# A fused attention and feed-forward kernel: order of the first loads, TensorE turns of two tiles, four equal token blocks and a new written-out order of work

## The chip, the cores and the metric

One core of a Trainium2 chip runs the whole kernel. The time is the device time of one execution in microseconds (us), the median of several runs.

## The reference

One pre-norm layer on 2048 tokens of width 640, in bfloat16. `A` is a linear attention of 32 heads of 20 columns, whose features are softmaxes of a projection and of its negative; `B` is a feed-forward layer of width 1536 whose gate is a plain product.

```python
def _A_ref(x, wqkv, w_phi, wo):
    q, k, v = heads(x @ wqkv)
    pq = jnp.einsum("bhsd,hdf->bhsf", q, w_phi)
    pk = jnp.einsum("bhsd,hdf->bhsf", k, w_phi)
    phi_q = jnp.concatenate([_softmax(pq), _softmax(-pq)], axis=-1)
    phi_k = jnp.concatenate([_softmax(pk), _softmax(-pk)], axis=-1)
    kv = jnp.einsum("bhsf,bhsd->bhfd", phi_k, v)
    z  = jnp.einsum("bhsf->bhf", phi_k)
    num = jnp.einsum("bhqf,bhfd->bhqd", phi_q, kv)
    den = jnp.einsum("bhqf,bhf->bhq", phi_q, z)[..., None] + 1e-6
    return merge(num / den) @ wo
def _B_ref(x, w_gate, w_up, w_down):
    return ((x @ w_gate) * (x @ w_up)) @ w_down
h = x + _A_ref(_layernorm(x), A_wqkv, A_w_phi, A_wo)
h2 = h + _B_ref(_layernorm(h), B_w_gate, B_w_up, B_w_down)
```

## The kernel before

The 2048 tokens are 16 tiles of 128, and the width 640 is five blocks of 128. All weights and the residual stay on chip. The code builds a graph of about a thousand named steps; each step has an engine, buffers that it reads and writes, and one entry in a written-out table, `PLAN`.

**What sets the order.** An entry such as `WTe1:7.329:1` or `V2:20.248::2` holds a start key, the choice of engine (0 the first named for the step, 1 the other) and the buffer slots, PSUM banks for TensorE's outputs. `arrange` (line 700) sorts each engine's steps by the key, and `emit` (line 717) derives the semaphore waits from the buffers. An engine runs its steps strictly in that order, so a step that waits holds all that stand behind it on its engine. DMAs stand in the order of the engine that issues them, SyncE (SP) or ScalarE (ACT).

**The steps by name** (a number is the tile; the lines are those of the profile):

- `x`, `wk`, `wv`, `w5` and the like are loads (line 285). A block of `wk` or `wv` is 128 rows of the key or value weights, 160 KB; `x0` to `x3` are one tile each, later loads of `x` two tiles. `wqt` is a transposing load of the query weights (309). `wg`, `wu`, `wd` and `wo` are the later weights.
- `warm` (371): products of zeros on TensorE at the start.
- `WT` turns a block of the key weights on TensorE (392), `WTe` copies it out (251). `F1` multiplies it by the feature weights `Phi` (411), so that a projection and its feature product become one matrix; `Fe` copies it out. `F0` does this for the query weights later.
- `L1s`, `L1a`, `L1l`, `L1e`, `L1n`, `xn`: the first layer norm (428 to 453). `LNG` names the tiles that share one pair of Ln and Exp (436, 439). `xt` turns the normed tile: on TensorE for the tiles in `TPE` (462, copied out by `xte`), by a DMA transpose on SyncE for the others (471).
- `V`, `K`, `Q`: projections (482), ten products a tile; for the tiles in `TSPLIT` they are five pieces by block of the weights. `Kx`, `Ks`, `Kr`, `Ke`, `Kn` make the key features (494 to 518, `Kn` on GpSimd); `KV` adds a tile to the sums (526), `KVe` masks the sums. `Qx`, `Qs`, `Qr`, `Qb`, `Qe`, `Qn` make the query features (553 to 571), `qT` turns them by DMA (576).
- `N`: numerator and denominator (589). `dd`, `rd`, `o`: the division on VectorE (600 to 606). `oT`: turned by DMA (610). `O`: output projection (616). `h`, `L2s`, `L2a`, `L2v`, `L2r`, `hc`: residual and second layer norm (620 to 639). `hT`: turned by DMA (643).
- `U`: gate and up products of a token block, for each of 12 blocks of width 128 (658); `g` copies the gate (663), `u` multiplies (666). `D`: down projection of a tile (677); `y`: scale and residual (689); `w`: store (691).

`FB` lists the token blocks of the feed-forward part. A block's `U` products need the `hT` of all tiles in it. `LASTCUT` cuts the last tile's `D` into pieces of columns.

Of the kernel before, what the change touches and what calls it, by code (L numbers as in the profile page):

```python
# [8 lines left out]
ALU = mybir.AluOpType  # L9
AX = mybir.AxisListType  # L10

P = 128
# [26 lines left out]
FB = [(0, 256), (256, 512), (768, 512), (1280, 512), (1792, 256)]  # L39
LNG = [[0], [1], [2, 3], [4, 5, 6, 7], [8, 9, 10, 11], [12, 13, 14, 15]]  # L40
TPE = (0, 1, 2, 3)
TSPLIT = (0, 1)
NWARM = 10
LASTCUT = [(0, 320), (320, 512), (512, 640)]
# [4 lines left out]
x0:0.7:1 w5:1.18:1 wk0:1.18 wv0:4.06 wk1:2.14 wv1:2.62 wk2:1.66:1 wv2:3.58:1 wk3:2.62:1 wv3:4.06 wk4:3.1 wv4:4.54:1 x1:0.7 x2:2.14:1 x3:1.66 x4:3.58:1  # L49
x6:3.1 x8:5.02:1 x10:5.02 x12:4.54:1 x14:21.015 wqt0:13.874 wqt1:9.289 wqt2:26.055 wqt3:6.94 wqt4:19.655 wo0:27.415 wo2:34.715 wd0:35.195 wd1:47.175  # L50
wd2:49.392 wd3:37.595 wg0:32.875 wu0:5.5 wg1:37.115 wu1:6.46 wg2:40.335 wu2:25.575 wg3:36.635 wu3:5.98 wg4:35.675 wu4:36.155 id0:0.9 gl0:1.2 eps:0.7
id1:1.45 gla0:2.07 glb0:2.51 gla4:2.29 glb4:4.51 gla1:2.73 glb1:3.17 gla2:3.39 glb2:4.73 gla3:1.85 glb3:2.95 va1:6.664 phz:3.61 ekz:6.364 rqz:6.064
Sz:7.734 mk0:6.164 mk1:7.484 mk2:7.934 zero:0.7 warm0:1.08 warm1:1.51 warm2:1.94 warm3:2.37 warm4:2.8 warm5:3.23 warm6:3.66 warm7:4.09 warm8:4.52::0
warm9:4.74 Ph0:4.95 Ph1:5.609 Ph2:5.743:1 WT0:4.96::1 WTe0:5.509 WT1:6.769::5 WTe1:7.329:1 WT2:5.836::0 WTe2:6.386 WT3:7.725::2 WTe3:8.85 WT4:8.886::0
WTe4:9.922 F1_0:6.342::6 Fe1_0:8.676:1 F1_1:8.162::4 Fe1_1:9.299 F1_2:7.219::0 Fe1_2:8.052:1 F1_3:9.509::6 Fe1_3:10.766 F1_4:10.953::0 Fe1_4:11.538:1
L1s0:3.993 L1a0:5.633 L1s1:4.813 L1a1:6.1 L1s2:7.03 L1a2:9.686 L1s3:6.21 L1a3:10.215 L1s4:11.145 L1a4:12.785 L1s5:11.965 L1a5:13.005 L1s6:13.115
L1a6:14.353 L1s7:10.325 L1a7:12.895 L1s8:20.053 L1a8:21.803 L1s9:20.983 L1a9:23.833 L1s10:14.463 L1a10:20.873 L1s11:15.283 L1a11:19.443 L1s12:28.423
L1a12:34.233 L1s13:25.363 L1a13:30.243 L1s14:26.183 L1a14:34.123 L1s15:31.773 L1a15:34.013 L1l0:6.132 L1e0:7.229 L1l1:7.009 L1e1:7.952 L1l2:10.546
L1e2:11.389 L1n2:11.899 L1n3:11.699 L1l4:14.835 L1e4:15.678 L1n4:16.588 L1n5:16.188 L1n6:16.388 L1n7:15.988 L1l8:24.376 L1e8:24.806 L1n8:28.209
L1n9:28.409 L1n10:25.45 L1n11:25.65 L1l12:34.675 L1e12:35.518 L1n12:35.895 L1n13:36.095 L1n14:38.854 L1n15:36.295 xn0:7.85::0 xt0:8.53::3 xte0:9.268:1  # L60
xn1:8.35::1 xt1:9.165::1 xte1:9.796:1 xn2:12.875:1:3 xt2:17.252::7 xte2:17.978 xn3:12.161:1:2 xt3:13.17::0 xte3:13.935:1 xn4:19.553::2 xt4:21.495
xn5:17.025:1:0 xt5:18.295 xn6:18.943::1 xt6:22.855 xn7:23.333::3 xt7:24.215 xn8:29.243::1 xt8:30.155 xn9:29.743::3 xt9:31.515 xn10:26.408:1:0
xt10:27.895 xn11:27.745:1:2 xt11:33.355 xn12:36.631:1:0 xt12:45.815 xn13:36.758::1 xt13:38.075 xn14:39.692::2 xt14:47.712 xn15:38.118:1:3 xt15:40.815
V0_0:14.536::0 V0_1:14.807 V0_2:15.079 V0_3:15.351 V0_4:15.622 Ve0:20.238::2 K0_0:9.866::2 K0_1:10.138 K0_2:10.681 K0_3:12.083 K0_4:12.898
Kx0_0:13.588::0 Kx0_1:15.055 Ks0:16.103::0 Kr0:17.738 Ke0:18.601 Kn0:18.961 KV0:21.606::0,1 V1_0:12.355::6 V1_1:13.449 V1_2:13.721 V1_3:13.992
V1_4:14.264 Ve1:15.778::0 K1_0:10.41::4 K1_1:11.268 K1_2:11.54 K1_3:11.811 K1_4:12.626 Kx1_0:14.211::1 Kx1_1:16.401 Ks1:17.523::1 Kr1:19.998
Ke1:22.731 Kn1:23.091 KV1:26.01 V2:20.248::2 Ve2:22.108::3 K2:18.89::6 Kx2_0:21.485::3 Kx2_1:22.881 Ks2:23.943::3 Kr2:25.545 Ke2:28.458 Kn2:28.818
KV2:31.759 V3:15.894::2 Ve3:18.751::1 K3:17.531::4 Kx3_0:19.375::2 Kx3_1:20.861 Ks3:21.913::2 Kr3:23.513 Ke3:24.596 Kn3:25.85 KV3:33.747 V4:24.651::6
Ve4:27.121::5 K4:26.325::4 Kx4_0:28.608::0 Kx4_1:29.471 Ks4:30.353::1 Kr4:32.115 Ke4:32.978 Kn4:33.536 KV4:36.051 V5:21.935::4 Ve5:23.753::4
K5:23.293::2 Kx5_0:24.921::4 Kx5_1:25.785 Ks5:27.003::0 Kr5:29.231 Ke5:30.095 Kn5:31.177 KV5:36.367 V6:32.074::6 Ve6:33.811::7 K6:30.4::4  # L70
Kx6_0:32.355::3 Kx6_1:33.188 Ks6:34.343::3 Kr6:36.391 Ke6:37.968 Kn6:39.054 KV6:43.561 V7:29.042::6 Ve7:30.868::6 K7:27.684::2 Kx7_0:30.245::1
Kx7_1:31.491 Ks7:32.593::2 Kr7:34.435 Ke7:35.618 Kn7:36.495 KV7:43.876 V8:34.063::4 Ve8:35.768::2 K8:38.671::2 Kx8_0:40.299::0 Kx8_1:41.132
Ks8:41.966::1 Kr8:43.566 Ke8:44.634 Kn8:45.961 KV8:48.538 V9:44.463::4 Ve9:46.092::0 K9:36.997::6 Kx9_0:38.831::2 Kx9_1:39.665 Ks9:40.498::0
Kr9:42.379 Ke9:43.242 Kn9:43.602 KV9:51.842 V10:49.125::6 Ve10:51.708:1:3 K10:46.093::2 Kx10_0:48.562::3 Kx10_1:49.455 Ks10:50.288::3 Kr10:51.925
Ke10:52.788 Kn10:53.419 KV10:56.233 V11:54.874::2 Ve11:57.303:1:1 K11:40.029::4 Kx11_0:41.756::4 Kx11_1:42.619 Ks11:43.452::2 Kr11:45.647 Ke11:49.305
Kn11:50.82 KV11:59.265 V12:63.655::2 Ve12:65.321:1:4 K12:56.548::4 Kx12_0:58.176::0 Kx12_1:59.01 Ks12:59.843::1 Kr12:61.48 Ke12:62.583 Kn12:63.355
KV12:73.164 V13:60.939::4 Ve13:63.15:1:5 K13:50.484::2 Kx13_0:52.165::1 Kx13_1:52.998 Ks13:53.92::0 Kr13:56.436 Ke13:57.479 Kn13:57.839 KV13:73.479
V14:67.73::2 Ve14:69.782:1:7 K14:65.014::4 Kx14_0:66.642::3 Kx14_1:67.529 Ks14:68.362::3 Kr14:70.209 Ke14:70.659 Kn14:71.163 KV14:73.795 V15:70.447::6
Ve15:72.075:1:6 K15:59.58::2 Kx15_0:61.84::2 Kx15_1:62.733 Ks15:63.901::2 Kr15:65.742 Ke15:66.192 Kn15:67.259 KV15:74.11 KVe0:74.956 KVe1:74.696
F0_0:35.421::6 Fe0_0:36.006:1 F0_1:36.682::4 Fe0_1:37.345 F0_2:35.736::2 Fe0_2:37.258:1 F0_3:33.432::2 Fe0_3:34.895 F0_4:38.356::4 Fe0_4:38.941:1  # L80
Q0_0:41.387::6 Q0_1:41.659 Q0_2:41.931 Q0_3:44.192 Q0_4:45.822 Qx0_0:46.715::1 Qx0_1:47.758 Qs0:48.772 Qr0:50.882::1 Qb0:53.179 Qe0:53.622 Qn0:56.018
qT0:57.473::1 Q1_0:47.452::4 Q1_1:47.723 Q1_2:47.995 Q1_3:48.267 Q1_4:48.854 Qx1_0:50.078::2 Qx1_1:51.122 Qs1:52.46 Qr1:54.589::2 Qb1:55.778
Qe1:57.869 Qn1:60.438 qT1:61.893::2 Q2:53.516::6 Qx2_0:55.633::4 Qx2_1:56.676 Qs2:58.054 Qr2:60.436::0 Qb2:61.743 Qe2:62.463 Qn2:65.714 qT2:67.169::4
Q3:42.202::2 Qx3_0:43.831::0 Qx3_1:44.844 Qs3:45.857 Qr3:47.518::0 Qb3:48.32 Qe3:49.185 Qn3:49.515 qT3:50.97::0 Q4:62.297::6 Qx4_0:63.925::0
# [153 lines left out]
def build_graph():  # L238
# [679 lines left out]
```

## Time and profile before

| | |
|---|---|
| median of 3 runs | 274.34 us (274.33 to 274.36) |
| span of the profiled execution | 272.2 us; the page has no other time for it |
| TensorE busy | 266.0 us, 2103 products |
| VectorE busy | 171.0 us |
| ScalarE busy | 116.6 us |
| GpSimd busy | 73.9 us |
| read and written in HBM | 11.00 MB and 2.62 MB |
| granted TensorE clock | 1.000 |

The span runs from the first to the last instruction. A matmul's duration in the profile includes its way through the array, so durations of neighbours overlap; the distance between two starts, or a piece of the chain divided by its count, is what one product costs. DMA-issuing instructions do not count as busy, though they occupy their engine's queue.

### The profile page before, as it was taken

Reading aid. Unit: us, or ns where it says so; the run is one execution under the profiler, and the core shown is the slowest. Engines: PE = TensorE matmul, PEld = TensorE weight load, DVE = VectorE, ACT = ScalarE, POOL = GpSimd, SP = SyncE. Lnnn points to the kernel's source line nnn. Section 1 sums busy time; section 2 is a strip of 40 time slices with the busy share of each in tenths; the row PEclk is TensorE's granted clock in tenths of the full one; section 3 lists DMA queues with packets and bytes.
Section 4 is the critical chain, followed back from the end, with each engine's and each line's share of the span. In section 5 each row is a group of like instructions: output and inputs, shape, how many; then the busy total and the mean of one; then the engine's idle time right before and its main releaser. Section 6 shows DMA issues by size and latency. Waiting matters only on the chain.

```text
span 272.2 us, 5234 instructions
## 1 busy us (share of the span) xinstructions
PE 266.0 (98%) x2103; PEld 177.2 (65%) x2103; DVE 171.0 (63%) x315; ACT 116.6 (43%) x307; POOL 73.9 (27%) x107
## 2 busy tenths in 40 slices
PE   7899999999989999999999999999999999999996
PEld 2777787777776788775555877766444457544774
DVE  4999978788899999897186147843324022314423
ACT  2999998987766746012213332300332220023000
POOL 7227996899974133200000000000000000000000
DMA  7997999987548998964022001531100001100011
GB/s 201 375 265 162 176 264 313 234 157 108 107 78 160 147 185 110 165 130 98 0 48 48 2 1 43 100 95 43 31 0 2 0 0 51 48 0 0 26 48 55
DMA packets 66600, 27.76 MB, mean 102 GB/s; under 512 B 57744, under 2 KB 65296, under 8 KB 66576
## 3 DMA queue, kind: packets, MB, share of 16 engines
q1 hardware_dynamic: 64752, 25.30, 45.2%
q10 hardware_dynamic: 1824, 2.13, 2.3%
q8 instruction: 16, 0.26, 0.5%
q14 instruction: 8, 0.07, 0.1%
HBM read 11.00 MB, written 2.62 MB: 50 GB/s over the span
## 4 chain that ended last, share of the span: by engine, by line
PE 93%; ACT 3%; DMA 2%; ACTq 1%; issue 0%; DVE 0%; DVEq 0%
PE ps L658 38%; PE ps L482 23%; PE ps L677 19%; PE ps L616 8%; DMA ev<-in_A_wqkv_dram 2%; PE ps L526 2%; ACT ph L553 2%; PE ps L589 1%; PE ps L411 1%; ACTq L285 1%; PE ps L462 0%; ACT ph L554 0%; PE ps L392 0%; ACT L884 0%; DVE Wp L689 0%
## 5 line engine op out<-in xcount | busy, mean ns | idle before, releaser
L658 PE MATMUL ps<-xnT,Wgu 128*128 128x512 bf16 (+1 forms) x600 | 105.2, 336 | 0.0
L658 PEld LDWEIGHTS ps<-xnT,Wgu 128*128 128x128 bf16 x600 | 58.5, 98 | 44.2 <-DVE ev L666 0.4
L663 ACT ACTIVATE gt<-ps 128x512 bf16<-128x512 f32 (+1 forms) x60 | 30.5, 511 | 91.4 <-PE ps L658 74.0
L482 PE MATMUL ps<-Wp,xnT 128*128 128x320 bf16 (+1 forms) x480 | 68.6, 299 | 0.8 <-ACT ph L554 0.8
L666 DVE TENSOR_TENSOR ev<-ps,gt 128x512 bf16<-128x512 f32 (+1 forms) x60 | 32.8, 577 | 47.4 <-PE ps L658 34.0
L482 PEld LDWEIGHTS ps<-Wp,xnT 128*128 128x128 bf16 x480 | 45.6, 97 | 18.4 <-ACT ph L554 0.9
L677 PE MATMUL ps<-Wd,ev 128*128 128x320 bf16 (+2 forms) x396 | 53.7, 295 | 0.0
L677 PEld LDWEIGHTS ps<-Wd,ev 128*128 128x128 bf16 x396 | 38.0, 98 | 14.5
L518 POOL TENSOR_TENSOR ek<-ek,SR 128x1280 bf16<-128x1280 bf16 x16 | 37.6, 2357 | 6.7 <-ACT SR L503 6.6
L689 DVE SCALAR_TENSOR_TENSOR Wp<-ps,rs,x_all 128x640 bf16<-128x640 f32 (+3 forms) x18 | 14.5, 808 | 32.9 <-PE ps L677 32.7
L553 ACT ACTIVATE ph<-ps 128x300 bf16<-128x300 f32 x64 | 23.8, 442 | 7.9 <-PE ps L482 7.4
L630 POOL TENSOR_SCALAR ln<-mv 128x1 f32<-128x1 f32 x16 | 3.3, 210 | 84.6 <-DVE mv L629 73.4
L557 DVE TENSOR_REDUCE S<-ph 128x66 f32<-128x1320 bf16 x16 | 24.2, 1515 | 3.1 <-ACT ph L554 3.1
L498 DVE TENSOR_REDUCE SR<-ek 128x64 f32<-128x1280 bf16 x16 | 23.4, 1472 | 1.3 <-ACT ek L494 1.2
L616 PE MATMUL ps<-Wo,Wp 128*128 128x320 bf16 x160 | 23.9, 299 | 0.3 <-ACT RQ L567 0.3
L494 ACT ACTIVATE ek<-ps 128x640 bf16<-128x640 f32 x32 | 22.3, 714 | 2.7 <-PE ps L482 2.4
L571 POOL TENSOR_TENSOR ph<-ph,RQ 128x660 bf16<-128x660 bf16 x16 | 20.9, 1307 | 6.2 <-ACT RQ L567 6.2
L639 ACT ACTIVATE xn<-x_all,mv 128x640 bf16<-128x640 bf16 x13 | 10.7, 828 | 24.2 <-DVE mv L629 24.2
L616 PEld LDWEIGHTS ps<-Wo,Wp 128*128 128x128 bf16 x160 | 15.2, 98 | 6.6 <-issue 0.6
L620 DVE TENSOR_TENSOR x_all<-ps,x_all 128x640 bf16<-128x640 f32 x16 | 13.0, 813 | 4.5 <-PE ps L616 4.4
L606 DVE TENSOR_TENSOR o<-ps,sm 128x720 bf16<-128x720 f32 x16 | 14.2, 894 | 0.1
L428 DVE BATCH_NORM_STATS2 st<-x_all 128x6 f32<-128x320 bf16 x16 | 7.6, 472 | 3.3 <-DMA x_all<-in_A_x_dram 3.3
(63 smaller groups left out, 171.4 us busy)
## 6 DMA issues: line engine op xcount, KB each, us to landing
out_dram<-Wp SPq DMA_DIRECT2D x15, 160.0 KB, 1.8
Wgu<-in_B_w_up_dram SPq DMA_DIRECT2D x5, 384.0 KB, 9.7
Wgu<-in_B_w_gate_dram SPq DMA_DIRECT2D x5, 384.0 KB, 7.0
Wd<-in_B_w_down_dram SPq DMA_DIRECT2D x4, 480.0 KB, 6.3
x_all<-in_A_x_dram SPq DMA_DIRECT2D x3, 320.0 KB, 6.8
x_all<-in_A_x_dram ACTq DMA_DIRECT2D x3, 320.0 KB, 9.1
Wp<-in_A_wqkv_dram SPq DMA_DIRECT2D x4, 160.0 KB, 7.4
x_all<-in_A_x_dram ACTq DMA_DIRECT2D x3, 160.0 KB, 4.9
```

What stands on the lines that cost most here:

```text
L482: ins = e.matmul(pb(b, hb)[:, 0:n1 - n0], lhsT=T["xnT"][:, NC - 1 - c, P * t:P * (t + 1)], rhs=T["Wp"][:, POS[kind], c, n0:n1], start=(c = ...
L494: G.op("act", "%sx%d_%d" % (nm, t, s), lambda e, s=s, b=b, ek=ek: e.activation(out=T["ek"][:, ek.slots[0], 0:2 * D].rearrange("p (b h s f) ...
L498: G.op("dve", "%ss%d" % (nm, t), lambda e, ek=ek, sr=sr: e.tensor_reduce(out=T["SR"][:, sr.slots[0], 0, :], in_=T["ek"][:, ek.slots[0], 0: ...
L518: G.op("pool", "Kn%d" % t, lambda e, ek=ek, sr=sr: e.tensor_tensor(out=T["ek"][:, ek.slots[0], 0:2 * D].rearrange("p (h f) -> p h f", f=DH ...
L553: e.activation(out=o_, in_=i_.rearrange("p (g j f) -> p g j f", j=3, f=DH), func=AF.Exp, scale=1.0 - 2.0 * sg)
L557: G.op("dve", "Qs%d" % t, lambda e, t=t, ph=ph: e.tensor_reduce(out=T["S"][:, t, 0:66].rearrange("p (g k) -> p g k", k=6), in_=pv(ph).rear ...
L571: return e.tensor_tensor(out=v, in0=v, in1=T["RQ"][:, rq.slots[0], 1, 0:33].rearrange("p (g j) -> p g j", j=3).unsqueeze(3).to_broadcast([ ...
L616: ins = e.matmul(pb(b, hb)[:, 0:320], lhsT=T["oT"][:, oT.slots[0], c, :], rhs=T["Wo"][:, c, 320 * hb:320 * (hb + 1)], start=(c == 0), stop ...
L658: ins = e.matmul(pb(b)[:, 0:n], lhsT=T["Wgu"][:, gu, c, P * ft:P * (ft + 1)], rhs=T["xnT"][:, NC - 1 - c, o0:o0 + n], start=(c == 0), stop ...
L663: G.op("act", "g%d_%d" % (bi, ft), lambda e, pg=pg, gt=gt, n=n: e.activation(out=T["gt"][:, gt.slots[0], 0:n], in_=pb(pg)[:, 0:n], func=AF ...
L666: o_ = G.op("dve", "u%d_%d" % (bi, ft), lambda e, pu=pu, gt=gt, hh=hh, ft=ft, n=n: e.tensor_tensor(out=T["hh"][:, hh.slots[0], ft, 0:n], i ...
L677: ins = e.matmul(pb(b, hb)[:, 0:w], lhsT=T["hh"][:, hh.slots[0], ft, P * tt:P * (tt + 1)], rhs=T["Wd"][:, ft, c0 + w * hb:c0 + w * (hb + 1 ...
```

## The change

- The first loads get a new order: `x1`, `w5`, `x0`, `wk2`, `wk3`, `wk0`, `x2`, `wk4`, `wv0`, `wk1`, `wv1`, `x4`, `wv2`, `x3`, `wv3`, `wv4`, then `wqt1`, `x8`, `x6`. All but `x1` and `x0` are issued by SyncE; before, ten of the first twenty came from ScalarE. `wu0`, `wu3` and `wu1`, which stood among the first loads, come after 38 in the keys.
- `warm` becomes eight products of 512 columns and five of 256; four of the five stand before the first `WT`, the last between the first `WT` and `xt1`.
- `TPE` shrinks from four tiles to two: tiles 2 and 3 are turned by DMA.
- `FB` becomes four blocks of 512 tokens; before there were blocks of 256, 512, 512, 512 and 256.
- `LNG` has nine groups for six. `LASTCUT` cuts at 320 and 576, and the piece of 256 columns comes last.
- `L1n`, `Kn`, `Qb`, `Qn` and `L2v` may run on VectorE as well as GpSimd. `PLAN` moves to VectorE: `Kn12`, `Qn3`, `Qn9`, six `Qb`, five `L1n` and eight `L2v`. Some copies change between ScalarE and VectorE: four `xn` and three `hc` go to VectorE, four `Ve` and three `Fe0` to ScalarE.
- `PLAN` is written anew: keys, engines and slots of all steps. After the last `KV` (tile 15), TensorE's order is `Q7 N0 N1 Q13 N3 N2 N9 Q11 O0 O1 Q14 O3 O2 Q8 N5 Q15 O9 N4 Q12 N7`, then the first `U` of block 0 (tiles 0 to 3). SyncE's order there is `qT10 oT0 oT1 qT4 oT3 oT2 oT9 qT7 hT0 hT1 hT3 hT2`.

```diff
-FB = [(0, 256), (256, 512), (768, 512), (1280, 512), (1792, 256)]
-LNG = [[0], [1], [2, 3], [4, 5, 6, 7], [8, 9, 10, 11], [12, 13, 14, 15]]
-TPE = (0, 1, 2, 3)
+FB = [(0, 512), (512, 512), (1024, 512), (1536, 512)]
+LNG = [[0], [1], [2], [3], [4, 5], [6, 7], [8, 9], [10, 11], [12, 13, 14, 15]]
+TPE = (0, 1)
 TSPLIT = (0, 1)
-NWARM = 10
-LASTCUT = [(0, 320), (320, 512), (512, 640)]
+NWARM = 8
+NFILL = 5
+LASTCUT = [(0, 320), (320, 576), (576, 640)]
...
+    for k in range(NWARM):
+        G.op("pe", "warm%d" % k, lambda e, k=k: e.matmul(T["PS"][:, 512 * k:512 * (k + 1)], lhsT=T["zero"][:, 0:P],
+             rhs=T["zero"][:, :], start=True, stop=True), 0.43, LT, [z_b], [], -90,
+             before=[G.by["warm%d" % j] for j in range(k)])
     wm_b = Buf("pwarm", "psum")
...
+    for k in range(NWARM, NWARM + NFILL):
+        G.op("pe", "warm%d" % k, lambda e: e.matmul(pb(wm_b)[:, 0:256], lhsT=T["zero"][:, 0:P], rhs=T["zero"][:, 0:256],
+             start=True, stop=True), 0.22, LT, [z_b], [wm_b], -89, before=[G.by["warm%d" % j] for j in range(k)])
+    wall = [G.by["warm%d" % k] for k in range(NWARM)]
...
-                    op1=ALU.mult), 0.2, LP, [rs_b[t], mv_b[t]], [nb_b[t]], 10 * t - 25)
+                    op1=ALU.mult), 0.2, LP, [rs_b[t], mv_b[t]], [nb_b[t]], 10 * t - 25, alts=[("dve", 0.07, LD)])
...
-            pool_c(1280), LP, [ek, sr], [ek], kk)
+            pool_c(1280), LP, [ek, sr], [ek], kk, alts=[("dve", dve_c(1280), LD)])
...
-        G.op("pool", "Qn%d" % t, qn, pool_c(660), LP, [ph, rq], [ph], kk)
+        G.op("pool", "Qn%d" % t, qn, pool_c(660), LP, [ph, rq], [ph], kk, alts=[("dve", dve_c(660), LD)])
```

## The prediction

> **What bounds the kernel now.** I read the page's busy times first, then TensorE's products by shape, TensorE's waits, the chain in order of time, and the timeline of the first 18 us and of 74 to 96 us.
>
> The page's first part, and two rows of the groups by shape (busy us, mean ns of one, idle before):
>
> ```profile
> PE 266.0 (98%) x2103; PEld 177.2 (65%) x2103; DVE 171.0 (63%) x315; ACT 116.6 (43%) x307; POOL 73.9 (27%) x107
> ```
>
> ```profile
> L658 PE MATMUL ps<-xnT,Wgu 128*128 128x512 bf16 x360 | 79.0, 379 | 0.0
> L658 PE MATMUL ps<-xnT,Wgu 128*128 128x256 bf16 x240 | 26.5, 273 | 0.0
> ```
>
> TensorE is the bound. Its means are latencies that overlap, so prices come from the chain in order of time (start, us, what, count), where back-to-back products show their pitch:
>
> ```profile
> 14.25 0.28 PE ps L462 x5
> ...
> 95.83 13.18 PE ps L658 x120
> ...
> 121.30 2.16 PE ps L658 x10
> ...
> 164.03 0.68 PE ps L677 x12
> ...
> 222.06 13.04 PE ps L677 x96
> ```
>
> A 256-token product costs 13.18/120 = 109.8 ns, a 512-token one 216 ns, a turned tile 0.28 us, a 640-wide down projection 3.26 us, a Q, K, V or O projection 1.36 us, an N or KV step 0.33 us, a fold 0.32 us. All real work, at these prices, is 259.7 us. The last product ends at 269.7, so TensorE loses 10 us, in two places.
>
> The head, from the timeline; the third column of a wait is what ended it:
>
> ```profile
> 8.66 0.28 PEld L392 LDWEIGHTS ps<-ident,ev 128*128 128x128 bf16 x5 [0.36 <-DMA ev<-in_A_wqkv_dram]
> ...
> 9.89 0.28 PEld L392 LDWEIGHTS ps<-ident,ev 128*128 128x128 bf16 x5 [0.34 <-DMA ev<-in_A_wqkv_dram]
> ...
> 10.78 1.25 PE L482 MATMUL ps<-Wp,xnT 128*128 128x320 bf16 x8
> ```
>
> The key weights' blocks arrive one by one, the last at 9.85 (the trace's landing events). When projections begin at 10.78, 5 weight turns, 4 folds and 2 token tiles are done: 1.40 + 1.28 + 0.56 = 3.24. **Head loss: 10.78 - 3.24 = 7.54 us.**
>
> The stage between the last KV step and the first feed-forward product:
>
> ```profile
> 77.38 1.18 PE L589 MATMUL ps<-KVm,scratch 128*128 128x63 bf16 x33
> 79.35 2.91 PE L482 MATMUL ps<-Wp,xnT 128*128 128x300 bf16 x20 [0.80 <-ACT ph L554]
> ...
> 84.31 1.52 PE L616 MATMUL ps<-Wo,Wp 128*128 128x320 bf16 x10
> 86.13 1.52 PE L616 MATMUL ps<-Wo,Wp 128*128 128x320 bf16 x10 [0.29 <-ACT RQ L567]
> ```
>
> Three N steps from 77.38 need 1.00, the next projection starts at 79.35: 0.97 lost. O from 84.31 needs 1.36, the next starts at 86.13: 0.46 lost. With smaller gaps at 82.6 (0.16), 92.4 (0.13), 92.9 (0.20) and 95.7 (0.07): **2.0 us**. At 35.24 another 0.17 goes, and nothing after 95.74. From there the time is the sum of products.
>
> **The sum.** The profiled span is 272.2 and the runs' median 274.34: 2.1 us lie around the span. I add differences of the span to the median.
>
> *Feed-forward blocks.* 240 products of 256 tokens (26.35 us) become 120 of 512 (25.92): **-0.43**, certain, since TensorE never waits there. Copies and multiplies of 512 columns (597 and 683 ns) fit under the 2.16 us of their two products.
>
> *Two tiles leave TensorE.* Two of 0.28: **-0.56**. Their two copies (0.40 us pitch on VectorE, 0.58 on ScalarE) go too. In their place SyncE turns tiles 2 and 3; a row of 2.7 us from issue to landing shows that price when nothing is queued. Whether V2 waits for tile 2 belongs to the head.
>
> *First loads in use order.* Loads land about in issue order: the seventh block of 160 KB at 7.76, the eighteenth at 12.72, or 0.45 us each. The last turned key block (wk4) was twelfth and becomes seventh, so it lands near 7.8 instead of 9.85; the last one now is wk1, ninth, near 8.7. Then two folds that stand ahead of V1: 8.7 + 0.28 + 0.64, so projections begin near 9.7, when 5 turns, 2 tiles and 3 folds (2.92) are done. Loss 6.8 instead of 7.5: -0.75. Against it: x1 landed at 3.57 and still cannot come sooner; tile 2's turn stands on SyncE behind the first transposing load of the query weights and x8 and x6, and V2 wants it near 9.7 + 6.1 = 15.8. By 0.45 us a block, the sixteenth lands at 11.8, that transposing load and four more blocks at about 14.3, tile 2 some 1 us later: a wait of 0 to 0.5. I take **-0.5** for the head, bounds -0.9 and +0.5.
>
> Nearly all loads now go through SyncE's queue instead of half through ScalarE's. Fourteen issues at 0.47 us end at 7.4, and blocks drain at 0.45, so issue is never far behind. The Trainium skill ("DMA: Bandwidth & Descriptors", "Issuing engines are not separate DMA queues") says that issuing from several engines saves only the issuing time, since all run on the same 16 engines; the trace's interleaved landings agree, and by the rule the term stands.
>
> *Zero products.* Eight of 512 and four of 256 columns at half rate (427 and 213 ns) last as long as the ten before (4.27 us); the fifth small one costs 0.11 between turns, while TensorE waits for loads anyway. The head's gaps of 0.57 and 0.69 us left the pitch at 56 ns, so keeping TensorE busy buys nothing either: **0**. Without the cover: +0.11.
>
> *New order, 76 to 96 us.* The first feed-forward block now needs tiles 0 to 3, not 0 and 1. TensorE's work between the last KV step and that block: 7 Q (9.52), 5 O (6.80), 8 N (2.67) = 19.0 us. SyncE must issue eleven transposes for it (oT of five tiles, two qT, hT of four), at pitches of 1.33 (oT and hT) and 1.6 (qT) in these rows: ten ahead of the last take 13.8. The first oT can go 3.4 us after the last KV step (0.84 for the two masks, 0.33 for N, 2.2 for the division on VectorE), and the last hT lands 2.65 after issue: 3.4 + 13.8 + 2.65 = 19.9. So at least 0.9 us must be lost; I take 1.5 against 2.0: **-0.5**, bounds -1.5 and +2. VectorE matters here: it is busy 19.8 of 20 us in 80 to 100, and gets a copy (0.46) and three or four small operations (0.1 each) from ScalarE and GpSimd.
>
> *Small operations moved off GpSimd* (one Kn, two Qn, six Qb, thirteen of one column), and three more Ln/Exp pairs (0.28 each on ScalarE): no row shows Kn on VectorE. Its bounds are the 1.4 us that the `o` multiply's pitch (0.81 for 720 columns) gives and GpSimd's own 2.31; I take 2. All lies beside TensorE's projections with slots ahead: 0; if the cover is gone, one Kn holds VectorE for 2 us, and the next key step with it.
>
> *Query weights.* F0 follows V8 at about 31.4 now, not 34.4, and needs all five transposed loads. The last is issued after nine turns (1.3 each) and five loads (0.55 each) from 11.6, at 26.1, and landed 3.65 to 5.8 later in rows of its kind: 29.8 to 31.9. **+0.2**, bounds -0.2 and +0.5.
>
> *The end.* The last piece grows from 192 to 256 columns, the early one shrinks from 128 to 64. Twelve of 64 cost 0.36 (a 63-column product: 30 ns) to 0.68, of 256 1.32, of 192 about 0.99, of 128 0.68: equal sums. The last addition grows by about 0.07 and its store by 0.05: **+0.1**.
>
> Sum: -0.43 - 0.56 - 0.5 - 0.5 + 0.2 + 0.1 = -1.7: span 270.5, **time 272.6**.
>
> **Rivals.**
> A. *Early transposes stall SyncE* (slower). The timeline shows two transposing loads holding SyncE for 6.94 us in all (2.62 and 4.27, by the trace), with loads queued ahead:
>
> ```profile
> 8.09 6.94 SPq L309 DMA_TRANSPOSE scratch<-in_A_wqkv_dram  x2
> ```
>
> Now one such load and then tiles 2, 4 and 5 meet queued loads. If the first holds 2.6 and the second 4.3, tile 2's issue ends at 15.8 and lands at 17.2, V2 waits 1.4; tile 4, held 3.25, lands near 21 and V4 waits 1.1 more. That takes the head's term from -0.5 to +2.2: 275.3. It decides as soon as tile 2 lands after V2's turn at 15.8. Against it: then three up-projection blocks of 384 KB stood ahead, now four blocks of 160. Chance 0.10. The Trainium skill ("VectorE: DVE Perf Modes", "Rules for kernel authors") prefers TensorE for a 128x128 transpose into PSUM, at 390 ns there against 1309 by DMA; by those figures ten squares would be worth 3.9 us on TensorE, while the trace's two tiles cost 0.56.
> B. *Four tiles before the first block* (about the same). If SyncE's qT pitches are the longest of that stage (1.7 and more) or VectorE delays a division, 1.9 us more is lost there: 274.4, within 0.2% of before. Speaking for it: VectorE at 99%. Against: more Q work covers it. Chance 0.12.
> C. *The head is no shorter*: reordered loads land in the same crowd, gain 0; the rest stands: 273.1. Chance 0.18.
> Forecast itself: 0.60.
>
> **Range and chances.** 0.2% is 0.55 us, about what a measurement of this kernel can tell from no change. Forecast and C are faster by more: 0.78; B within: 0.12; A slower: 0.10. The bounds of head and stage together reach from 271.2 upwards; B's 274.4 is taken in, A left out: 271.2 to 274.5.
>
> **What would show it.** Right: first projection at 9.5 to 10; no waits of L482 on tile 2; the chain with 512-token products alone; TensorE's losses at 76 to 96 near 1.5; the last product near 268. Wrong: a wait of L482 on xnT's DMA at 15 to 20, of L411 on the query weights at 31, of L658 on xnT at its first product, or gaps of several tenths that recur through 20 to 73 us, where the old order lost only 0.17 and all engines are busy.

## The result and the profile after

**280.97 us** (median of 4 runs, 280.23 to 281.95) against 274.33 before on the same chip: the ratio is 1.0251, with a 95% interval of 1.0227 to 1.0275. The forecast was 272.6. The profiled execution took 281.95, the longest of the four, with a span of 280.2; I compare it with before's 272.2 and keep in mind that about 1 us of its 8.0 is this execution's own.

What the forecast called certain is there. The first part of the page after:

```profile
PE 267.9 (96%) x1976; PEld 165.3 (59%) x1976; DVE 182.7 (65%) x324; ACT 114.8 (41%) x300; POOL 67.9 (24%) x85
```

TensorE's products by shape, and a piece of its chain in order of time (start, us, what, count):

```profile
L651 PE MATMUL ps<-xnT,Wgu 128*128 128x512 bf16 x480 | 107.2, 379 | 1.1 <-DMA xnT<-xn 0.6 <-DVE sm L592 0.5
```

```profile
174.68 14.03 PE ps L651 x65
```

All gate and up products have 512 columns and cost 14.03/65 = 215.8 ns. But VectorE's busy time grew by 11.7 us, while the operations moved to it from GpSimd are some 6 us long when they run alone (the lengths are measured below); in this execution their rows add up to 14.1 us. This is the first thing to notice on the page. The second is where TensorE waits. Its waits (waited for: us, times, longest):

```profile
PE ps L474 <- ACT ek L486: 2.6, 1, 2.6
PE ps L474 <- DMA xnT<-xn: 2.5, 3, 1.0
...
PE ps L474 <- DVE ev L242: 0.8, 1, 0.8
PE ps L651 <- DMA xnT<-xn: 0.6, 1, 0.6
```

L474 is the projection (482 before), L242 a copy out of PSUM (251), L486 the exponential `Kx` (494): the last two hold a bank that the next projection needs. Before, projections lost 0.17 us between 20 and 73 us. TensorE's timeline shows the places; the bracket is the idle time ahead of a piece and what ended it:

```profile
9.20 1.25 PE L474 MATMUL ps<-Wp,xnT 128*128 128x320 bf16 x8
...
17.05 3.16 PE L474 MATMUL ps<-Wp,xnT 128*128 128x320 bf16 x22 [0.98 <-DMA xnT<-xn]
...
29.26 2.89 PE L474 MATMUL ps<-Wp,xnT 128*128 128x320 bf16 x20 [0.49 <-DMA xnT<-xn]
33.16 1.53 PE L474 MATMUL ps<-Wp,xnT 128*128 128x320 bf16 x10 [1.01 <-DMA xnT<-xn]
...
58.65 1.52 PE L474 MATMUL ps<-Wp,xnT 128*128 128x320 bf16 x10 [0.84 <-DVE ev L242]
...
73.33 7.29 PE L474 MATMUL ps<-Wp,xnT 128*128 128x300 bf16 x40 [2.61 <-ACT ek L486]
...
86.66 0.49 PE L581 MATMUL ps<-KVm,scratch 128*128 128x63 bf16 x11 [0.38 <-DVE sm L592]
...
90.48 1.52 PE L608 MATMUL ps<-Wo,Wp 128*128 128x320 bf16 x10 [0.38 <-ACT RQ L552]
```

Measured from start to start, as in the prediction: V1's pieces lose 0.61 us at 11 to 12.4 (they wait for the value weights), V2 1.15, V7 0.65, V8 1.18, K13 1.01 and Q6 2.77; the stage from 82 to 103 us loses 2.15 (2.0 before), and the second token block 0.78 at 137.6. After Q6's wait the products of 300 columns run at half rate for some 3 us, which costs 1.5 more. Projections begin at 9.20 with 2.92 us of work done, a head loss of 6.28 where it was 7.54.

**Balance.** Less work -1.0, head -1.26, waits behind the head +8.4 (10.5 now, 2.1 before), half rate +1.5: +7.6. The last product starts at 277.25 for 269.41, +7.84.

The same execution shows a cause for K13 and Q6. VectorE at 54 and 74 us, each time with GpSimd at the same time behind it:

```profile
54.45 0.60 DVE L445 TENSOR_SCALAR xn<-x_all,mv,rs 128x640 bf16<-128x640 bf16 x1
54.97 2.80 DVE L563 TENSOR_TENSOR ph<-ph,RQ 128x660 bf16<-128x660 bf16 x1
```

```profile
54.71 2.36 POOL L510 TENSOR_TENSOR ek<-ek,SR 128x1280 bf16<-128x1280 bf16 x1
57.02 1.91 POOL L563 TENSOR_TENSOR ph<-ph,RQ 128x660 bf16<-128x660 bf16 x1
```

```profile
73.58 1.47 DVE L490 TENSOR_REDUCE SR<-ek 128x64 f32<-128x1280 bf16 x1
74.97 3.42 DVE L510 TENSOR_TENSOR ek<-ek,SR 128x1280 bf16<-128x1280 bf16 x1
```

```profile
74.69 5.92 POOL L510 TENSOR_TENSOR ek<-ek,SR 128x1280 bf16<-128x1280 bf16 x2
```

Qn3 (54.97) and Kn12 (74.97) are two of the moved operations. Both begin beside a scaling on GpSimd, which ends at 57.07 (54.71 + 2.36) and 77.0; both end 0.7 and 1.4 us behind that, at 57.77 and 78.39. And GpSimd's next one, begun when the first ended, is longer by as much: Qn2 1.91 for its usual 1.31, and Kn15, the second of the last pair, about 3.6 (5.92 for the two) for 2.36. It looks as if the two engines exclude each other in operations with two inputs from SBUF, while a sum or a norm (one input) runs freely.

From there Q6's wait can be followed back. VectorE, then ScalarE:

```profile
66.46 2.47 DVE L563 TENSOR_TENSOR ph<-ph,RQ 128x660 bf16<-128x660 bf16 x1
68.85 1.29 DVE L556 TENSOR_TENSOR RQ<-RQ 128x32 f32<-128x32 f32 x1
```

```profile
70.17 0.23 ACT L559 ACTIVATE RQ<-RQ 128x32 f32<-128x32 f32 x1 [2.01 <-DVE RQ L556]
71.57 0.26 ACT L493 ACTIVATE SR<-SR 128x64 f32<-128x64 f32 x1 [1.17 <-DVE SR L490]
...
71.99 1.27 ACT L486 ACTIVATE ek<-ps 128x640 bf16<-128x640 f32 x2
```

Qn9 and Qb1, moved operations both, end late on VectorE; ScalarE has idled 2.01 us for Qb1's result, and behind that step stand Kr14 and, last, the exponentials of K15, which end at 73.27 and free the bank for Q6 at 73.33. K13's bank was freed by Ve10, which stood behind Qn3.

### The profile page after: what moved, and what is told of

It is laid out like the page before. It is cut to its first block, busy times and chain, and to the rows that moved or that the text cites. A ratio compares the mean times of both kernels' runs of the same rounds, so it can differ in the third digit from the quotient of the medians.

```text
span 280.2 us, 4952 instructions
## 1 busy us (share of the span) xinstructions
PE 267.9 (96%) x1976; PEld 165.3 (59%) x1976; DVE 182.7 (65%) x324; ACT 114.8 (41%) x300; POOL 67.9 (24%) x85
## 4 chain that ended last, share of the span: by engine, by line
PE 70%; DVE 14%; DMA 7%; ACT 6%; SPq 1%; issue 1%; DVEq 0%; ACTq 0%
PE ps L651 35%; PE ps L670 19%; PE ps L474 8%; DMA xnT<-xn 6%; PE ps L608 6%; DVE S L549 3%; ACT ph L545 3%; DVE SR L490 2%; DVE ph L563 2%; DMA ev<-in_A_wqkv_dram 1%; SPq L276 1%; ACT ek L486 1%; PE ps L581 1%; DVE x_all L612 1%; PE ps L518 1%
## 5 line engine op out<-in xcount | busy, mean ns | idle before, releaser
L651 PE MATMUL ps<-xnT,Wgu 128*128 128x512 bf16 x480 | 107.2, 379 | 1.1 <-DMA xnT<-xn 0.6
L651 PEld LDWEIGHTS ps<-xnT,Wgu 128*128 128x128 bf16 x480 | 46.4, 98 | 54.0 <-issue 1.5
L474 PE MATMUL ps<-Wp,xnT 128*128 128x320 bf16 (+1 forms) x480 | 71.2, 303 | 6.1 <-ACT ek L486 2.6
L656 ACT ACTIVATE gt<-ps 128x512 bf16<-128x512 f32 x48 | 28.0, 596 | 91.4 <-PE ps L651 66.2
L474 PEld LDWEIGHTS ps<-Wp,xnT 128*128 128x128 bf16 x480 | 45.8, 99 | 26.5 <-DMA xnT<-xn 4.4
L659 DVE TENSOR_TENSOR ev<-ps,gt 128x512 bf16<-128x512 f32 x48 | 31.9, 682 | 38.0 <-PE ps L651 23.1
L486 ACT ACTIVATE ek<-ps 128x640 bf16<-128x640 f32 x32 | 20.6, 699 | 1.4 <-PE ps L474 1.4
L563 POOL TENSOR_TENSOR ph<-ph,RQ 128x660 bf16<-128x660 bf16 x14 | 19.3, 1390 | 7.2 <-ACT RQ L559 7.2
L632 ACT ACTIVATE xn<-x_all,mv 128x640 bf16<-128x640 bf16 x11 | 9.1, 826 | 18.0 <-DVE mv L621 9.5
L556 POOL TENSOR_TENSOR RQ<-RQ 128x32 f32<-128x32 f32 x10 | 2.3, 238 | 38.1 <-ACT RQ L552 38.1
L622 POOL TENSOR_SCALAR ln<-mv 128x1 f32<-128x1 f32 x8 | 1.5, 211 | 40.6 <-DVE ln L622 26.3
```

The source lines that it names most:

```text
L474: ins = e.matmul(pb(b, hb)[:, 0:n1 - n0], lhsT=T["xnT"][:, NC - 1 - c, P * t:P * (t + 1)], rhs=T["Wp"][:, POS[kind], c, n0:n1], start=(c = ...
L486: G.op("act", "%sx%d_%d" % (nm, t, s), lambda e, s=s, b=b, ek=ek: e.activation(out=T["ek"][:, ek.slots[0], 0:2 * D].rearrange("p (b h s f) ...
L563: return e.tensor_tensor(out=v, in0=v, in1=T["RQ"][:, rq.slots[0], 1, 0:33].rearrange("p (g j) -> p g j", j=3).unsqueeze(3).to_broadcast([ ...
L651: ins = e.matmul(pb(b)[:, 0:n], lhsT=T["Wgu"][:, gu, c, P * ft:P * (ft + 1)], rhs=T["xnT"][:, NC - 1 - c, o0:o0 + n], start=(c == 0), stop ...
L656: G.op("act", "g%d_%d" % (bi, ft), lambda e, pg=pg, gt=gt, n=n: e.activation(out=T["gt"][:, gt.slots[0], 0:n], in_=pb(pg)[:, 0:n], func=AF ...
L659: o_ = G.op("dve", "u%d_%d" % (bi, ft), lambda e, pu=pu, gt=gt, hh=hh, ft=ft, n=n: e.tensor_tensor(out=T["hh"][:, hh.slots[0], ft, 0:n], i ...
```

## Experiments

There are three theories: **P**, the exclusion; **D**, transposes that land late behind loads; **R**, the new order leaves GpSimd's chain (16 `Kn` of 2.31 us, with `Qn` and `Qb` between) no slack, so that whatever delays it delays the last `KV`. A ratio is to the kernel before in the same job, in brackets its 95% interval. The start of KVe0, the mask on the finished key-value sums, serves as a mark of GpSimd's chain: 76.45 before, 82.04 after. GpSimd's idle time from the start of its first `Kn` to the end of its last is a second mark: 6.1 us before, 13.1 after. The rows of `Kn`, before and after, show how much GpSimd idles right ahead of a `Kn`, the first one included (last figure):

```profile
L518 POOL TENSOR_TENSOR ek<-ek,SR 128x1280 bf16<-128x1280 bf16 x16 | 37.6, 2357 | 6.7 <-ACT SR L503 6.6
```

```profile
L510 POOL TENSOR_TENSOR ek<-ek,SR 128x1280 bf16<-128x1280 bf16 x15 | 36.4, 2439 | 9.8 <-ACT SR L495 9.8
```

The runs were made on several chips; on these the kernel before took 274.09 to 274.75. The diffs below show only the entries and lines that matter. Places in time come from one profiled execution of each kernel.

### Undoing parts of the change

**e1.** The nine operations back on GpSimd.

```diff
-Kn12:67.028:1 Qn3:51.438:1 Qn9:60.309:1 Qb0:57.282:1
+Kn12:67.028 Qn3:51.438 Qn9:60.309 Qb0:57.282
```

(and Qb1, Qb8, Qb9, Qb13, Qb15 likewise)

> The changed kernel with nine two-input operations (Kn12, Qn3, Qn9, six Qb) back on GpSimd; all else, keys and slots too, as changed. Theory P: these operations on VectorE wait for whatever two-input operation GpSimd is in, so VectorE runs late from 55 us on; TensorE's waits of 1.0 us at 58.7 and 2.8 us at 73.3, and the half-rate products behind the second (1.7 us), come from that. P expects 275.5 to 277.5, no TensorE gap over 1 us between 50 and 80, and a granted clock of 1.00 at 70 to 80. Theory D: late DMA turns at 17, 29 and 33 us (3.0 us together) push everything behind; D expects that the time stays within 1 us of 281, since those waits stay. Theory R, the new order is too tight for GpSimd as well as for VectorE: the waits at 55 to 80 move to other steps and less than 2 us is gained.

Measured 282.26, 1.0284 [1.0239, 1.0329]: no gain, rather a loss. Q6 waits 1.20 for 2.77 and its products run at full clock, but K12, KV12 and KV15 now wait 0.79, 1.10 and 1.28, and KVe0 starts at 81.34. What VectorE gets back, GpSimd loses: it is busy for 47.5 us between its first and last `Kn`, where it was 44.5. P alone falls, as R said.

**e2.** Tile 2 on TensorE again.

```diff
-TPE = (0, 1)
+TPE = (0, 1, 2)
-xt2:11.368
+xt2:11.60::2 xte2:11.83
```

> The changed kernel with tile 2 turned on TensorE between two V pieces and copied out by ScalarE; tile 3 stays on DMA. D expects the wait of 1.15 us for tile 2 at 17 us gone, VectorE's and ScalarE's key steps as much earlier, and 279 to 280 us or less. P expects that the wait at 17 us goes and the time does not follow, 280 to 281.5, since VectorE's late stretch at 55 to 75 us sets the end of the key stage.

Measured 280.63, 1.0243 [1.0204, 1.0282]. V2's wait is gone, K3 waits 0.56 us instead, and Q6 still 2.78: the 1.1 us do not come out at the end.

**e3.** SyncE issues the transpose of tile 7 one transposing load earlier, and that of tile 8 ahead of a load of gate weights and of x14.

```diff
-xt7:23.151 wg0:24.46 x14:24.941
+xt7:21.0 wg0:27.5 x14:27.6
```

> The changed kernel with the turn of tile 7 issued one transposing load earlier, and the loads of wg0 and x14 issued behind the turn of tile 8 and the last transposing load. D expects the waits of 0.65 us for tile 7 at 29 us and of 1.2 us for tile 8 at 33 us gone, and 279 us. P expects those two waits gone and 280 to 281.5 us, for the reason given for tile 2.

Measured 280.53, 1.0252 [1.0203, 1.0302]. V7 and V8 no longer wait (1.83 us), V6 waits 0.59, Q6 2.77, and the time is the same within the intervals. D alone falls too.

**e4.** All three.

> The three edits together: nine two-input operations on GpSimd, tile 2 on TensorE, turns of tiles 7 and 8 ahead of wg0 and x14. If P and D each hold for their part, 272.5 to 274.5, below the kernel before; if only P holds, 275.5 to 277.5; if R, 278 or more.

Measured 280.3, 1.0232 [1.0177, 1.0287]. Even together they bring next to nothing (the interval is wide). KVe0 starts at 79.83, 3.4 us behind before's. The early waits for transposes are gone but for V6, which now waits 1.28 us. From 62 to 80 us TensorE waits 4.6 us in five places: 2.4 of it for key scalings on GpSimd, the rest for copies and banks that come late from ScalarE. This is what R said.

### GpSimd's chain

**g1, g2.** `Kn` on half of its columns, in the kernel after and in the one before; half of the key features stay unscaled.

```diff
-out=T["ek"][:, ek.slots[0], 0:2 * D]
+out=T["ek"][:, ek.slots[0], 0:D]
```

> The kernel after, with GpSimd's scaling of the key features done on the first half of its columns only (the second half of the key features stays unscaled, a part of the computation that is left out). Theory G (GpSimd's chain of key and query scalings, entered late and held up by ScalarE, sets the last key-value step and through it the stage from 70 us on): the sixteen key scalings fall from 2.3 to about 1.2 us each, the copy of the finished key-value sums starts near 76 instead of 82 us, the wait of 2.77 us of Q6 at 73.3 and the throttled products after it go, and the time is 274.5 to 277. Theory D (transfers behind later loads cost it): GpSimd's speed changes little, the waits at 17, 29, 33 us stay and the stage from 70 us on keeps its loss: 280 to 281. Theory R (the order on TensorE is short of ready work whichever engine is the quicker): 278 to 281, with the same waits at other pieces.

> The kernel before with the same half of the key scaling left out. Theory G with before at its edge: 49.4 us of GpSimd's work between 19.7 and 74.1 us were just enough, so TensorE, which lost only some 2 us to waits in all, wins 0 to 1.5 us: 272.8 to 274.4. If GpSimd's chain had been the bound of before as well, the time falls by 3 us or more.

Measured 277.02, 1.0104 [1.0089, 1.0119], and 274.23, 1.0006 [0.9993, 1.0018]. The row of `Kn` in g1:

```profile
L510 POOL TENSOR_TENSOR ek<-ek,SR 128x640 bf16<-128x640 bf16 x15 | 19.6, 1308 | 17.9 <-ACT SR L495 17.9
```

The same relief is worth 4 us to the kernel after and nothing to the kernel before: GpSimd's speed is on the path of the one and not of the other. In the kernel after it also shortens Kn12 on VectorE, and with it the exclusion. But g6 below and e4 differ by the halving alone and have none of these operations on VectorE, and there it is worth 5.2 us (280.3 to 275.1). Q6's wait falls to 0.88, KVe0 comes at 77.31, and the clock stays full. The waits at 17, 29 and 33 us stay, 2.8 us in all, and are now the largest.

**g4.** The kernel before with 3.0 us more on GpSimd, between Kn0 and Kn1.

```diff
-phz:3.61
+phz:19.0
+        e.memset(v[:, 0:2, 0:10, 0:120], 0.0)
```

> The kernel before, with GpSimd's first zeroing of the padding moved between its key scalings 0 and 1 and lengthened by 2400 columns of zeros (about 2.4 us by the rate of the zeroing rows, 528 columns in 0.54 us; with the moved part 3 to 3.5 us). It delays GpSimd's chain by about 3 us near 22 us and touches nothing else. Theory G: its 5 us of idle time between 19.7 and 74 us take up only a part, the copy of the key-value sums starts 0 to 3 us later than 76.5, and the kernel is slower by 0.5 to 4 us: 274.8 to 278. Rival (GpSimd has slack enough, and the change lost its time by the order on TensorE and the transfers alone): 274.2 to 274.6.

Measured 274.21, 0.9989 [0.9966, 1.0011]: nothing. The added zeroing took 2.10 us by its row and the moved part 0.84, and GpSimd's idle time between its first and last scaling shrank from 6.1 to 3.6. My theory of a kernel before "at its edge" was wrong: its order holds at least 2 us of slack. (The profiled execution is the longest of the eleven, 275.51; its projections begin 1.3 us later than before's, and KVe0, at 77.95, 1.5.)

**g5, g6.** The halved kernel after with e2's and e3's edits (g5), and with e1's too (g6).

> The kernel after with half of GpSimd's key scaling left out (as before, the second half of the key features stays unscaled), and in addition tile 2 turned on TensorE again and SyncE issuing the transposes of tiles 7 and 8 ahead of the load of a gate block and of x14. With GpSimd's chain out of the way (277.0 us without these two edits), theory D gets its own test: the waits of 1.09, 0.54 and 1.16 us for tiles 2, 7 and 8 go, 0.28 us for turning tile 2 and about 0.6 us for a later wait of V6 come: 275.2 to 276. If the late turns had cost nothing of their own, the time stays at 277.

> As the run before it, and also the nine two-input operations back on GpSimd, which has over 20 us of idle time between its key scalings in the halved form. Theory P: with room on GpSimd, taking them off VectorE frees the steps behind them (the key scaling 12 alone held VectorE for 3.4 us, the query scalings 3 and 9 for 2.5 to 2.8): another 0.5 to 2 us, 273.5 to 275. If these operations cost nothing on VectorE: no difference from the run before it.

Measured 275.51, 1.0065 [1.0041, 1.0090], and 275.10, 1.0026 [1.0006, 1.0045]. With GpSimd out of the way, the late turns cost 1.1 (by the ratios) to 1.5 us (by the medians) of their own: D is real, it was hidden behind R. The moved operations then still cost 0.4 to 1.1, less than most of what I had put, and the two intervals overlap a little. These figures compare runs of two chips (g1 and g5) and of one chip (g5 and g6).

**m1.** What feeds GpSimd late? ScalarE's row in the kernel after, 33 to 36 us:

```profile
34.73 0.71 ACT L242 ACTIVATE ev<-ps 128x640 bf16<-128x640 f32 x1 [1.24 <-PE ps L474]
35.33 0.39 ACT L493 ACTIVATE SR<-SR 128x64 f32<-128x64 f32 x2
```

The copy Ve8 waits 1.24 us for the projection V8, which waits for its tile's transpose; behind it stand Kr5 and Kr4, whose sums on VectorE ended at 32.42 and 31.03, and GpSimd idles 4.0 us ahead of Kn4. In m1, which is e4 with a further edit, such small steps go ahead:

```diff
-Kr0:20.904 Ke0:21.195 Kr4:32.169 Ke4:33.722 Kr5:32.023 Ke5:35.036 Ke7:38.197
+Kr0:19.66 Ke0:19.70 Kr4:29.30 Ke4:29.33 Kr5:31.40 Ke5:31.42 Ke7:33.60
-Ke6:42.315 Ke11:50.66 Kn11:51.054 Ke9:52.52 Kn9:54.633
+Ke6:38.95 Ke11:43.22 Kn11:46.0 Ke9:45.42 Kn9:46.3
```

> The kernel of the run with all three undone (two-input operations back on GpSimd, tile 2 on TensorE, transposes of tiles 7 and 8 first; 280.3 us), with one more edit: ScalarE's small steps that release GpSimd (Kr and Ke of tiles 0, 4, 5, and Ke of 6, 7, 9, 11) are moved ahead of the copies and exponentials of other tiles that they stood behind, and GpSimd takes key scalings 11 and 9 ahead of 8 and of two query steps. Theory (GpSimd's chain, 9 us of idle time between its first and last key scaling in that run, is fed late by ScalarE's order): the first key scaling starts near 21 instead of 22.2, some 2 to 3 us of the idle time go, the last key-value step comes 1 to 3 us sooner, and so does the end: 277.5 to 279.5. Rival (the steps on GpSimd are short of TensorE's projections, so that what comes sooner only waits longer): 280.

Measured 277.52, 1.0119 [1.0096, 1.0142], 2.8 us less than e4 by the medians and 3.1 by the ratios, though e4's interval alone is 1.5 us wide to each side. The row of `Kn` in e4 and then in m1; the last figure is the idle time ahead of it and what ended it:

```profile
L511 POOL TENSOR_TENSOR ek<-ek,SR 128x1280 bf16<-128x1280 bf16 x16 | 37.5, 2355 | 8.0 <-ACT SR L496 7.8
```

```profile
L511 POOL TENSOR_TENSOR ek<-ek,SR 128x1280 bf16<-128x1280 bf16 x16 | 37.5, 2357 | 5.0 <-ACT SR L496 5.0
```

So the order on ScalarE counts, and not only the projections: apart from Kn11 and Kn9 on GpSimd itself nothing else was moved. `Kn` waits 3 us less in all, but other operations on GpSimd wait more, so that its idle time from first to last `Kn` hardly falls (9.5 to 9.3); what shows in the traces is a chain that begins 1.0 us sooner (22.22 to 21.22) and a KVe0 that comes 1.2 us sooner (79.83 to 78.68). Where the rest of the 2.8 us comes from stays open.

### The exclusion by itself

**g3.** The kernel before with the nine operations on VectorE and no other edit.

> The kernel before with nine two-input operations of GpSimd written for VectorE instead, as the change does (key scaling 12, query scalings 3 and 9, six query shift products), and no other edit. Theory P (a two-input operation on VectorE does not run beside one on GpSimd but waits for its end): the moved scalings take 2 to 3.4 us on VectorE wherever GpSimd is in one of its own, and the kernel gets slower by 0.5 to 3 us: 274.8 to 277. The rival (GpSimd is the engine that is short, and what leaves it is a relief): 273.5 to 274.4. Theory of the prediction (all of it lies beside TensorE): 274.2 to 274.6.

Measured 278.98, 1.0172 [1.0156, 1.0189]: +4.9 us, more than I had put. Here one part of the change alone loses three quarters of what the whole loses. GpSimd gets no relief from it: it idles 16.6 us between its first and last scaling where it idled 6.1, since VectorE's sums `Ks`, which feed it, come late. VectorE has hardly a gap from 50 to 80 us; Qn3 takes 2.50 us there, and Qb0 1.42 for some 0.2.

**k1, k2.** Is that the moved work on a full engine, or the exclusion? The kernel before gets seven extra operations on VectorE, at the places of seven of the nine and of about their sizes, and nothing is moved; they are sums in k1 and products in k2:

```diff
+            return e.tensor_reduce(out=T["dumi"][:, 0:g], in_=a, axis=AX.X, op=ALU.add)
```

```diff
+            return e.tensor_tensor(out=T["gt"]..., in0=a,
+                                   in1=T["dumi"][:, 0:g].unsqueeze(2).to_broadcast([P, g, DH]), op=ALU.mult)
```

> The kernel before, with seven extra operations on VectorE and nothing moved: one-input sums over a tile of x, as long as the moved operations are alone (660, 1280 and 80 columns: about 0.75, 1.4 and 0.15 us), at the places in VectorE's order which the moved query scalings 3 and 9, key scaling 12 and four shift products have. Together about 3.5 us of added work on VectorE. If the cost of the moved operations is VectorE's own load: 276 or more, as most of the 4.8 us that moving them cost. If it is the exclusion between VectorE and GpSimd: each takes its own length whatever GpSimd does, and the time is 274.3 to 275.5.

> The same seven extra operations at the same places and of the same sizes, but as products of two inputs (the tile of x and a vector repeated along the head's columns, the form of the key scaling), into a tensor that nothing reads then. Exclusion: each that starts beside one of GpSimd's scalings waits for its end (up to 2.3 us) and GpSimd's next one waits for it, so the two kernels differ by 1 to 4 us: 275.5 to 279. Load alone: the same time as with one input, within 0.5 us.

Measured 275.26, 1.0028 [0.9999, 1.0058], and 277.69, 1.0099 [1.0069, 1.0130]. VectorE's rows of k1, then of k2 (busy us, mean ns):

```profile
L452 DVE TENSOR_REDUCE dumi<-x_all 128x33 f32<-128x660 bf16 x2 | 1.7, 831 | 0.0
...
L452 DVE TENSOR_REDUCE dumi<-x_all 128x64 f32<-128x1280 bf16 x1 | 1.5, 1476 | 0.0
L452 DVE TENSOR_REDUCE dumi<-x_all 128x4 f32<-128x80 bf16 x4 | 0.9, 226 | 0.0
```

```profile
L455 DVE TENSOR_TENSOR gt<-x_all,dumi 128x1280 bf16<-128x1280 bf16 x1 | 2.9, 2902 | 0.0
L455 DVE TENSOR_TENSOR gt<-x_all,dumi 128x80 bf16<-128x80 bf16 x4 | 2.5, 623 | 0.0
L455 DVE TENSOR_TENSOR gt<-x_all,dumi 128x660 bf16<-128x660 bf16 x2 | 2.3, 1130 | 0.0
```

As sums they keep their length whatever GpSimd does (each of the seven ran beside a product on GpSimd, and equal ones took equal times), and cost the kernel 0.6 us (interval 0 to 1.6). As products they take 3.6 us more in all, and lengthen GpSimd's `Kn` from 2355 to 2432 ns in the mean and `Qn` from 1305 to 1382 (2.4 us in all). The product of 1280 columns ended 1.35 us behind the scaling on GpSimd that it met (71.15 and 69.80). The kernel pays 2.4 us more than with sums by the medians, 1.9 by the ratios. The exclusion is shown. Load and exclusion together cost 3.0 us here; the rest of g3's 4.9 no run takes apart. The Trainium skill ("SBUF — State Buffer", "SBUF: two separate sides") states this rule: VectorE with two SBUF inputs and GpSimd reading SBUF take one port pair as an exclusive lock, whichever starts first, for the whole instruction. The rows agree.

### The new parts under another order

**r1 to r4.** All of the computation and all parts of the change, with `PLAN` chosen anew from the measured pitches (r1, r3 and r4 with tile 2 on TensorE). r1 and r2 still took the exclusion to hold up VectorE alone.

> All of the computation, with the change's parts (loads in use order, zero products, four blocks of 512 tokens, tile 2 turned on TensorE too) and a table PLAN whose order, engines and slots are chosen anew from the pitches measured in the two traces, with two rules that these runs gave: a two-input feature operation on VectorE starts beside none on GpSimd, and ScalarE's small steps for GpSimd do not stand behind copies that wait for a late tile. Theory (P and R, an order that is too tight for GpSimd and VectorE, and not the change's new parts): the work on TensorE is 0.7 us less than before, the head's loss 1.1 us less, the other waits about the same 2 us: 272 to 273.5. If the new parts themselves cost the time (transposes of tiles 2 and 3 by DMA, the loads' order, four tiles before the first block): 277 or more.

> As the run before it, but with tiles 2 and 3 turned by DMA as in the change, and another such order. Theory as there: 271.8 to 273.5, with no wait of V2 for tile 2 if its transpose no longer stands behind the loads of x6 and x8; 1 us more if it still does.

> As the first new order (tile 2 on TensorE, all of the computation), with the rule as the rows of that run gave it: two-input operations of VectorE and GpSimd exclude each other in both directions (Kn on VectorE took 1.90 us and lengthened GpSimd's Kn14 from 2.36 to 3.60). In that order the last key-value step waited 1.41 us for GpSimd and later products waited 0.47 and 0.71 us for transposes; here none of these is planned. Theory: 1.5 to 2.5 us less than the first new order, 273 to 274.2, the kernel before or a little better. If the new parts cost something that no wait shows, it stays at 275.

> As the run before it with another order of the same kind (the first key scaling planned some 2 us sooner, other scalings on VectorE). Theory: 273 to 274.2, within 0.5 us of the run before it. A difference of more than 1 us between the two would mean that the time hangs on small shifts of transfers which the orders do not control.

Measured 275.44, 1.0048 [1.0029, 1.0067]; 277.44, 1.0116 [1.0089, 1.0143]; 274.84, 1.0013 [0.9987, 1.0040]; 275.11, 1.0012 [0.9993, 1.0031]. With tile 2 on TensorE (r1, r3, r4) a new order is worth 5.5 to 6.1 us, and the kernel stands beside the one before: r1 is 0.5% slower, r3 and r4 cannot be told from it. With tiles 2 and 3 both turned by DMA, as in the change (r2), a new order is worth 3.5 us, and 1.2% are still lost. That is in the range that I had given to a cost of the new parts themselves; since r2 is also another order, and its projections begin only at 11.29 (10.78 before), the runs do not decide what of it is the parts. None of the four is faster than before. In r1 Kn12 on VectorE started at 67.72 and took 1.90, Kn14 on GpSimd at 68.24, and now it was GpSimd's that was held: 3.60 us for 2.36. Where my expectation failed (272 to 274.2 for all four): the head did not give its 1.1 us each time. r1 and r3 have the same first ten loads; the projections began at 9.12 in the one and at 10.37 in the other, and the same block of key weights, issued at 1.72 and 1.73, landed at 6.03 and 7.43. And r3 loses 4.4 us behind the head in eight waits of 0.37 to 1.10, where before loses 2.1. Whether an order exists that keeps the change's 1.0 us of saved work (0.7 with tile 2 on TensorE) and beats the kernel before stays open.

## Why the prediction was wrong

Two steps failed. The first is *Small operations moved off GpSimd*: "All lies beside TensorE's projections with slots ahead: 0". Alone, in the kernel before, moving the nine two-input operations measured +4.9 (g3). My bounds for one `Kn` on VectorE, 1.4 and 2.31, were taken from rows of each engine on its own: 1.48 is what Kn12 took in g3, and 3.42 beside GpSimd's. I asked what an operation costs and whether TensorE waits for it, and not whether VectorE and GpSimd can run it at the same time.

The second, and the larger one in the whole, is a term that the sum put at nothing. *New order* was priced for 76 to 96 us alone. There it was near: 2.15 measured for 82 to 103, 1.5 forecast, so rival B (3.4 lost, by its 274.4) did not happen. For 20 to 73 us I wrote down no term at all; the last sentence says only that the old order lost 0.17 there. The new one loses 5.6 us there in four waits, and 1.5 to the half rate behind the last of them: some 7 us of the 9.4 by which the profiled execution missed the forecast. The small loss of the old order was earned by slack for GpSimd, which g4 measured, and the new order has none, as the relief in g1 shows: GpSimd's first `Kn` starts 3.25 us later (22.97 for 19.72) and it idles 13.1 us on the way for 6.1. The wait shows on TensorE at 58 and 73 us, far from where it arises. My last sentence named the sign to look for; I did not turn it into a rival with a price.

By its other steps:

- *Blocks*, -0.43, and *two tiles leave TensorE*, -0.56: there.
- *Head*: better than forecast up to the first projection (-1.26 for -0.75), then 0.61 lost on the value weights and 1.15 on V2, where I allowed 0 to 0.5. Net +0.5, the upper bound. The -1.26 is in part luck: 9.20 is the earliest start of projections among the nine kernels with this order of first loads, and the others began at 9.46 to 9.78. Tile 2's transpose was issued at 10.93 and landed at 17.00: 6.1 us and not the 2.7 of an empty queue, behind x8 (14.07) and x6 (16.41).
- *Rival A* came close to tile 2's landing (17.2 forecast, 17.00 measured) by the wrong mechanism. SyncE was not stalled: the first transposing load held it 1.21 us and not 2.6, and no issue held it longer than 1.66 up to 40 us. The transpose was issued early and landed late, behind loads that were already issued. V2 waited as A said (1.15 us for 1.4), V4 did not, but V7 and V8 did, 1.83 us. Tile 7's transpose stood behind two transposing loads, tile 8's behind a gate block and x14 (issued at 26.99, landed at 33.11). A's end on the slower side was right in sign and held a tenth of the chance.
- *Zero products, query weights, the end*: no wait of L403 on the query weights and no loss at the end; nothing here against the 0, +0.2 and +0.1.

The causes do not add up. Removing the moved operations (e1), the late turns (e2, e3) or all three (e4) moves the time by +1.3 to -0.7 us; after GpSimd is relieved (-4.0), the turns bring 1.1 to 1.5. ScalarE's order brings 2.8, a whole new order 3.5 with the change's turns and 5.5 to 6.1 with tile 2 on TensorE. Late transposes hold V7 and V8, these hold their copies on ScalarE, these hold `Kr`, this holds `Kn`; and the offload that should have given GpSimd room gave it none: from the start of its first `Kn` to the end of its last it took 54.4 us before and 57.6 after.

## What to carry to other kernels

Price a move from one engine to another by what the two do at the same time, and before calling it hidden measure the slack of the chain that the receiving engine feeds; here a relief (g1, g2) and a delay (g4) of the suspected engine told slack from none in three runs. When a whole order is new, sum it stage by stage, each engine's chain from its first to its last operation, however small the old order's waits are. If undoing each part alone brings nothing, look for an engine that all of them delay.

## What the runs showed of the hardware

- A product of two inputs from SBUF on VectorE and one on GpSimd exclude each other for their whole length, in both directions (2902 ns in k2 for 1476 of an equal sum in k1; GpSimd's 3.60 us for 2.36 in r1). In the kernel before, sums of 1280 columns (1.43 to 1.49 us) and norms of 640 (0.55 to 0.60) took the same on VectorE beside a product on GpSimd as alone. So did the multiply `o`, a product with one input in PSUM (0.86 to 0.91 both ways). Copies out of PSUM took 0.81 to 0.83 beside one, and 0.81 alone in g3.
- After Q6's wait of 2.77 us the granted clock was 0.57 in the kernel after from 73 to 77 us; the same wait gave 0.61 in e3 (71 to 75 us) and 1.00 in e2 (73 to 77). The row of the stretches (us, busy times, then granted clock, DMA share, GB/s):

```profile
73.00:77.00 4.00, 3.67 (x15) 2.13 (x16) 4.00 (x3) 2.66 (x11) 4.00 (x4) 0.57 0.65 122
```

  The Trainium skill ("TensorE: Matmul & The Clock Gate", "What's actually happening") puts the fall to half rate after an idle window of about 3.4 us; here it came after a wait of 2.8, in two executions of three.
- The same load, issued at the same time in the same order, lands up to 1.0 us apart from one execution to the next: the block `wk4`, issued at 3.28 in e1 and at 3.29 in e2, landed at 6.69 and at 7.73. That is nearly as much as the head had to gain.
